# A fifth of two FFN weights placed on partitions 0 to 63 and loaded by eight of the sixteen DMA engines, in a decode kernel that is bound by its DMA engines

## The chip, the cores and the metric

The kernel runs on one core of a Trainium2 chip. The metric is the device time of one execution in microseconds (us). Where a ratio is given, it is the mean time of one kernel's fast runs over that of the other kernel's fast runs of the same rounds on the same chip, so it is not quite the ratio of the medians quoted beside it.

## The reference

One decode step of a parallel block: attention over the last 2,048 positions of a K and a V cache, plus a gated FFN, plus the residual. Everything is bf16.

```python
# x [4,1,640]; k_cache, v_cache [4,32,8192,192]; wq [640,6144]; wo [6144,640]
# w1, w3 [640,1536]; w2 [1536,640]; window W = 2048
xn = layernorm(x)
out = x + attention(xn @ wq, k_cache[:, :, -W:], v_cache[:, :, -W:]) @ wo \
        + (silu(xn @ w1) * (xn @ w3)) @ w2
```

The data is 223 MB, nearly all K and V, read once. There is little arithmetic per byte.

## The kernel before

All loads are issued from one queue (SP), in program order. K tiles have two buffers, V tiles three; wq borrows the V buffers at the start. VectorE (DVE) multiplies K by the broadcast query, TensorE (PE) adds up by matmul with the identity, and so on. The parts that matter here:

```python
def load_k(h):                      # 128 partitions x 24,576 bytes
    kt = kpool.tile([P, NJ, Dh], BF16, tag="kt")
    nc.sync.dma_start(out=kt[:].rearrange("q j d -> q (j d)"),
                      in_=k_win[:, h].rearrange("b (p j) d -> p b (j d)", p=PB))
# ... load_v alike
def x_load():                       # x a second time, for the residual
    xr["t"] = const.tile([B, D], BF16, name="x_res")
    nc.sync.dma_start(out=xr["t"][:], in_=A_x.rearrange("b s d -> (b s) d"))
# ...
def ffn_load(name, w):              # w1, w3: 128 partitions x 5 rows of 3,072 bytes
    wt = fpool.tile([P, KC, F], BF16, tag="w", name=name)
    nc.sync.dma_start(out=wt[:].rearrange("p k n -> p (k n)"),
                      in_=w.rearrange("(p kc) n -> p (kc n)", kc=KC))
def ffn_in(name):
    for kc in range(KC):
        for w in range(HG):         # 4 column groups of 32
            nc.tensor.matmul(ffn["ps"][w*CT:(w+1)*CT, :], lhsT=xnT[:, kc]...[:, 0:CT],
                             rhs=ffn[name][:, kc, w*FW:(w+1)*FW], ...)
# schedule: w1 loaded in head 6, w3 in head 8; a slot is a quarter of a head
add(f, 0, ffn_load, "w1", B_w1)     # f = 6 * 4
add(f + 8, 0, ffn_load, "w3", B_w3)
```

Of the kernel before, what the change touches and what calls it, by code (L numbers as in the profile page):

```python
# [11 lines left out]
BF16 = mybir.dt.bfloat16  # L12
# [6 lines left out]
def kernel(  # L19
# [20 lines left out]
    nc = tc.nc  # L40
    P = 128
    B, Sq, D = A_x.shape
    _, H, Sk, Dh = A_k_cache.shape
    W = min(4096, max(256, Sk // 4))
    F = B_w1.shape[1]
    KC = D // P
# [9 lines left out]
    CT = 32  # L56
# [3 lines left out]
    N0 = D // 2  # L60
    QC = 512
    NQ = H * Dh // QC
    assert D % P == 0 and F % QC == 0 and P % B == 0 and W % (PB * GQ) == 0
    assert JQ * DD == 512 and JQ % 2 == 0 and 2 * Dh <= 512 and 2 * N0 == D and N0 <= 512
    assert (H * Dh) % QC == 0 and NQ % 6 == 0 and QW % P == 0 and Dh == CT * RPP and P == HG * CT and F == HG * CT * FC
    assert 2 * H * Dh <= NJ * Dh and KBUFS == 2 and VBUFS == 3
# [3 lines left out]
    fpool = ctx.enter_context(tc.tile_pool(name="ffn", bufs=1))  # L70
# [3 lines left out]
    const = ctx.enter_context(tc.tile_pool(name="const", bufs=1))  # L74
# [5 lines left out]
    ps_t = ctx.enter_context(tc.tile_pool(name="ps_t", bufs=1, space=MemoryType.PSUM))  # L80
# [29 lines left out]
    x_sb = const.tile([B, D], BF16, name="x_sb")  # L110
# [3 lines left out]
    for k0 in range(0, KC, 2):  # L114
        n = min(2, KC - k0)
        wt = vpool.tile([P, 2, H * Dh], BF16, tag="vt")
        nc.sync.dma_start(out=wt[:, 0:n, :].rearrange("p k n -> p (k n)"),
                          in_=wq_v[:, k0:k0 + n, :].rearrange("p k n -> p (k n)"))
# [4 lines left out]
    idb = const.tile([P, P], BF16, name="idb")  # L123
# [38 lines left out]
    xn = const.tile([B, D], BF16, name="xn")  # L162
# [6 lines left out]
    xnT = const.tile([P, KC, PB, B], BF16, name="xnT")  # L169
    nc.vector.tensor_copy(out=xnT[:], in_=xnT_ps[:].unsqueeze(2).to_broadcast([P, KC, PB, B]))  # L170


    qbc = const.tile([P, H * Dh], BF16, name="qbc")
    for c0 in range(0, NQ, 6):
        qps = [pool.tile([P, QC], FP32, tag=tag, name="qps")
               for pool, tag in ((ps_add, "ps"), (ps_add, "ps"), (ps_o, "o_ps"), (ps_o, "o_ps"), (ps_m, "mt"), (ps_t, "t"))]
        for kc in range(KC):
            for i, qp in enumerate(qps):
                nc.tensor.matmul(qp[:], lhsT=xnT[:, kc].rearrange("p a b -> p (a b)"),  # L179
                                 rhs=wq_rows[kc][:, (c0 + i) * QC:(c0 + i + 1) * QC],  # L180
                                 start=(kc == 0), stop=(kc == KC - 1))
# [17 lines left out]
    def acc_half(i, lhsT, rhs, first=False, last=False):  # L199
        nc.tensor.matmul(acc[i * CT:i * CT + B, :], lhsT=lhsT, rhs=rhs[:, i * N0:(i + 1) * N0], start=first, stop=last)  # L200
# [3 lines left out]
            acc_half(i, lhsT, rhs, last=last)  # L204

    po = ps_po.tile([P, Dh + 1], FP32, name="po")
    xr = {}

    def x_load():
        xr["t"] = const.tile([B, D], BF16, name="x_res")  # L210
        nc.sync.dma_start(out=xr["t"][:], in_=A_x.rearrange("b s d -> (b s) d"))

    def x_add(i):
        acc_half(i, idb[0:B, 0:B], xr["t"], first=True)

    def mult(u):
        h, g = u // GQ, u % GQ
# [106 lines left out]
    FW = F // HG  # L324
# [3 lines left out]
    ffn = {}  # L328

    def ffn_load(name, w):  # L330
        wt = fpool.tile([P, KC, F], BF16, tag="w", name=name)
        nc.sync.dma_start(out=wt[:].rearrange("p k n -> p (k n)"), in_=w.rearrange("(p kc) n -> p (kc n)", kc=KC))
        ffn[name] = wt

    def ffn_in(name):
        ffn["ps"] = ps_t.tile([P, FW], FP32, tag="t", name="f_ps")
        for kc in range(KC):
            for w in range(HG):
                nc.tensor.matmul(ffn["ps"][w * CT:(w + 1) * CT, :], lhsT=xnT[:, kc].rearrange("p a b -> p (a b)")[:, 0:CT],
                                 rhs=ffn[name][:, kc, w * FW:(w + 1) * FW], start=(kc == 0), stop=(kc == KC - 1))  # L340

    def ffn_silu():
        nc.scalar.activation(out=sT[:], in_=ffn.pop("ps")[:], func=ACTF.Silu)
# [23 lines left out]
    def add(slot, phase, fn, *args):  # L367
        sched[slot].append((phase, len(sched[slot]), fn, args))
# [31 lines left out]
    e = ends[H - 1][1] + 1  # L400
    for hg in range(NG - 2):
        a = ((hg + 1) * HG - 1) * GQ + L + 3
        add(hg * HG * GQ + 8, 0, wo_load, hg)
        add(a, 6, ge_proj, hg, 0, RPP // 2)
        add(a + 1, 6, ge_proj, hg, RPP // 2, RPP)
    f = FFN_HEAD * GQ
    add(f, 0, ffn_load, "w1", B_w1)
    add(f + 7, 7, ffn_in, "w1")
    add(f + 7, 9, ffn_silu)
    add(f + 8, 0, ffn_load, "w3", B_w3)  # L410
    add(f + 15, 7, ffn_in, "w3")
    add(f + 15, 9, ffn_h)
    add(8, 0, x_load)
    add(16, 6, x_add, 0)
    add(17, 6, x_add, 1)


# [53 lines left out]
```

## Time and profile before

| | before |
|---|---|
| median of the first runs | 529.32 us |
| span of the profiled execution | 527.6 us |
| DMA | 423 GB/s mean, 9 tenths busy or more in all slices but two |
| PE, DVE busy | 67%, 65% |

First, lines of the profile page of the kernel before: the busy time of each engine (PEld is TensorE loading weights, ACT is ScalarE, POOL is GpSimd); the DMA share in tenths over 40 equal slices of the span and what the engines moved; the DMA queues (packets, MB, share of the time of 16 engines); and the chain of work that ended last, by line.

```profile
PE 353.5 (67%) x2306; PEld 142.6 (27%) x2307; DVE 345.6 (65%) x435; ACT 45.6 (9%) x143; POOL 1.1 (0%) x8
DMA  8999999999999999999999999999999999999994
GB/s 358 434 430 415 420 439 434 430 434 419 439 438 427 432 427 437 429 434 428 432 432 432 432 427 435 432 432 430 432 430 432 432 430 434 429 435 427 438 419 203
q1 hardware_dynamic: 11680, 222.97, 98.6%
q8 instruction: 18, 0.29, 0.2%
q14 instruction: 5, 0.04, 0.0%
DMA kt<-in_A_k_cache_dram 54%; DVE pr L219 15%; PE ps L230 9%; PE po L307 4%; DVE sc L238 3%; DMA wt<-in_A_wq_dram 3%; PE qps L179 2%; PE o_ps L282 2%; DVE z L274 1%; ACT ex L266 1%; PE mt L260 1%; DVE oT L315 1%; DVE og L312 0%; PE acc L200 0%; ACT L266 0%
```

The kernel's own queue q1 fills 98.6% of what sixteen engines have, and the chain is mostly waits for K tiles. So no engine of the core but the DMA engines limits it. The two "instruction" queues look negligible by bytes. They are not: they don't fall evenly on the sixteen engines.

Now the timeline of the kernel before at four places (start in us, length, engine, line, operation, and in brackets the idle time before it and what ended it): where PE starts on wq, where DVE starts on the last K tile, one matmul group of the tail, and the last matmuls and the last DVE instruction.

```profile
10.70 4.89 PE L179 MATMUL qps<-wt,xnT 128*128 128x512 bf16 x12 [2.35 <-DMA wt<-in_A_wq_dram]
498.64 1.76 DVE L219 TENSOR_TENSOR pr<-kt,qbc 128x3072 bf16<-128x3072 bf16 x1 [2.71 <-DMA kt<-in_A_k_cache_dram]
513.82 2.73 PE L282 MATMUL o_ps<-vt,z 128*8 128x384 bf16 x32
523.86 0.71 PE L200 MATMUL acc<-w,hT 128*4 128x320 bf16 x8
524.62 0.48 DVE L437 CAST res<-acc 36x320 bf16<-36x320 f32 x1 [1.62 <-PE acc L200]
```

After the last K tile there are still 25 us of DMA (V, wo, w2) and 26 us of compute, side by side.

**A view that the argument needs.** The trace also records every DMA packet and every increment of a DMA's semaphore (the counter by which an engine that waits learns that a load has landed). A K load has sixteen increments in the trace of before, the second load of x (four rows) has four. Each is taken here as one engine's share landing: three of the increments come 2.52, 2.67 to 2.69 and 2.80 to 2.82 us after the first in each of the loads that land from 481, 488 and 495 us on. A tile counts as landed at the last one (DVE starts on the last K tile at 498.64 us, 0.02 us after its last increment). For the last K tile of the kernel before, in us after the first engine:

```
first engine 495.43:  0  0.25 0.26 0.26 0.36 0.39 0.77 | 2.52 2.68 2.81 3.08 3.08 3.10 3.11 3.11 3.20   -> lands at 498.62
```

Seven engines are early, nine late. All sixteen had started level, within 0.5 us at 43 us. What holds nine back can be followed in the packets: when q8 brings one of its 18 packets of 16 KB (0.88 to 0.97 us each), one engine loses about 1.45 us (the packet itself, and 0.45 to 0.55 us by which the data packet beside it gets longer than its 912 ns). Eight engines take turns in this. A ninth gets three packets of 8 KB on q14 and loses about 0.8 us by each (0.31 us for the packet, 0.53 or 0.54 us by which a data packet gets longer). These packets keep step with the program: q8 brings 18 for 4,613 instructions of PE and PEld, one for about 256, and the three of q14 come when 50, 178 and 303 of DVE's recorded instructions have begun. This is why they are called "DVE fetches".

### The profile page before, as it was taken

The numbers are of one execution on the slowest core, as the hardware profiler recorded it, in microseconds if no ns is written. First come the engines' busy times: TensorE is split into PE (matmuls) and PEld (weight loads), VectorE is DVE, ScalarE is ACT, GpSimd is POOL, SyncE is SP. The second block draws the span as 40 slices with busy tenths as digits, with TensorE's granted clock in tenths as the row PEclk, the third lists the DMA queues.
The fourth block names the chain that finished last, engine by engine and source line by source line (L and its number), as shares of the span: only waits on it lengthen the run. The fifth ranks groups of instructions, "written<-read, shape, count | busy, mean of one in ns | idle before, by whom it ended". The sixth has DMA issues, their size and how long they took to land.

```text
span 527.6 us, 5428 instructions
## 1 busy us (share of the span) xinstructions
PE 353.5 (67%) x2306; PEld 142.6 (27%) x2307; DVE 345.6 (65%) x435; ACT 45.6 (9%) x143; POOL 1.1 (0%) x8
## 2 busy tenths in 40 slices
PE   2865886765657476577637866577566777675686
PEld 0322332322212232223212322223222332232233
DVE  3179775776458567686637876577657867677661
ACT  2111000100211000000000000000000000000010
POOL 0000000000000000000000000000000000000000
PEclk9889887899878989789997998789997988799788
DMA  8999999999999999999999999999999999999994
GB/s 358 434 430 415 420 439 434 430 434 419 439 438 427 432 427 437 429 434 428 432 432 432 432 427 435 432 432 430 432 430 432 432 430 434 429 435 427 438 419 203
DMA packets 11719, 223.31 MB, mean 423 GB/s; under 512 B 1312, under 2 KB 1328, under 8 KB 2608
## 3 DMA queue, kind: packets, MB, share of 16 engines
q1 hardware_dynamic: 11680, 222.97, 98.6%
q8 instruction: 18, 0.29, 0.2%
q14 instruction: 5, 0.04, 0.0%
q10 hardware_dynamic: 16, 0.01, 0.0%
HBM read 222.96 MB, written 0.01 MB: 423 GB/s over the span
## 4 chain that ended last, share of the span: by engine, by line
DMA 57%; DVE 22%; PE 18%; ACT 2%; issue 1%; SPq 0%
DMA kt<-in_A_k_cache_dram 54%; DVE pr L219 15%; PE ps L230 9%; PE po L307 4%; DVE sc L238 3%; DMA wt<-in_A_wq_dram 3%; PE qps L179 2%; PE o_ps L282 2%; DVE z L274 1%; ACT ex L266 1%; PE mt L260 1%; DVE oT L315 1%; DVE og L312 0%; PE acc L200 0%; ACT L266 0%
## 5 line engine op out<-in xcount | busy, mean ns | idle before, releaser
L230 PE MATMUL ps<-pr,idb 128*128 128x512 bf16 x768 | 208.5, 412 | 152.3 <-DVE pr L219 152.3
L219 DVE TENSOR_TENSOR pr<-kt,qbc 128x3072 bf16<-128x3072 bf16 x128 | 223.5, 1746 | 113.9 <-DMA kt<-in_A_k_cache_dram 113.9
L230 PEld LDWEIGHTS <-idb 128*128 128x128 bf16 x768 | 74.4, 102 | 258.7 <-issue 200.1
L238 DVE TENSOR_REDUCE sc<-ps 128x16 f32<-128x512 f32 x128 | 87.2, 681 | 2.0 <-PE ps L230 2.0
L282 PE MATMUL o_ps<-vt,z 128*8 128x384 bf16 x1024 | 60.6, 373 | 2.7 <-DMA vt<-in_A_v_cache_dram 2.7
L307 PE MATMUL po<-o_sb,sel_w 128*32 128x192 f32 x128 | 49.1, 517 | 1.1 <-ACT o_sb L289 1.1
L282 PEld LDWEIGHTS <-z 128*8 128x8 bf16 x1024 | 26.2, 94 | 32.8 <-issue 22.8
L289 ACT COPY o_sb<-o_ps 128x384 f32<-128x384 f32 x32 | 15.3, 479 | 189.7 <-PE o_ps L282 189.7
L274 DVE TENSOR_TENSOR z<-ex,mask_b 128x256 bf16<-128x256 bf16 x32 | 13.5, 422 | 22.0 <-ACT ex L266 22.0
L263 ACT COPY negm<-mt 128x1 f32<-128x1 f32 x32 | 5.1, 159 | 259.0 <-PE mt L260 259.0
L307 PEld LDWEIGHTS po<-o_sb,sel_w 128*32 128x32 f32 x128 | 13.6, 128 | 26.8 <-issue 25.0
L179 PE MATMUL qps<-wt,xnT 128*128 128x512 bf16 x59 | 17.2, 456 | 4.8 <-DMA wt<-in_A_wq_dram 4.7
L185 DVE CAST qbc<-qps 128x512 bf16<-128x512 f32 x6 | 3.8, 684 | 18.7 <-PE qps L179 18.7
L260 PEld LDWEIGHTS mt<-ones_ff,gneg 1*128 1x128 f32 x64 | 9.5, 186 | 13.8 <-issue 11.7
L252 DVE TENSOR_REDUCE gmax<-mt 1x4 f32<-1x128 f32 x32 | 8.8, 275 | 6.6 <-PE mt L247 6.6
L260 PE MATMUL mt<-ones_ff,gneg 1*128 1x1 f32 x64 | 12.2, 258 | 0.0
L247 PE MATMUL mt<-idf,lmax 128*1 128x128 f32 x32 | 10.6, 330 | 1.1 <-DVE lmax L242 1.1
L266 ACT ACTIVATE ex<-sc,negm 128x64 bf16<-128x64 f32 x32 | 11.1, 348 | 1.0
L179 PEld LDWEIGHTS <-xnT 128*128 128x128 bf16 x60 | 6.7, 112 | 14.8 <-issue 9.7
L200 PE MATMUL acc<-wo_t,oT 128*4 128x320 bf16 x96 | 9.2, 298 | 0.4 <-DVE oT L315 0.4
L294 PEld LDWEIGHTS po<-rsum,tot_w 128*32 128x32 f32 x64 | 4.6, 110 | 14.1 <-issue 12.5
L242 DVE TENSOR_REDUCE lmax<-sc 128x1 f32<-128x64 f32 x32 | 7.0, 220 | 1.1
(52 smaller groups left out, 64.2 us busy)
## 6 DMA issues: line engine op xcount, KB each, us to landing
kt<-in_A_k_cache_dram SPq DMA_DIRECT2D x32, 3072.0 KB, 19.0
vt<-in_A_v_cache_dram SPq DMA_DIRECT2D x31, 3072.0 KB, 26.1
wo_t<-in_A_wo_dram SPq DMA_DIRECT2D x8, 960.0 KB, 20.5
wt<-in_A_wq_dram SPq DMA_DIRECT2D x2, 3072.0 KB, 13.3
w<-in_B_w_dram SPq DMA_DIRECT2D x2, 1920.0 KB, 27.1
vt<-in_A_v_cache_dram SPq DMA_DIRECT2D x2, 1536.0 KB, 31.2
wt<-in_A_wq_dram SPq DMA_DIRECT2D x1, 1536.0 KB
w<-in_B_w_dram SPq DMA_DIRECT2D x1, 1280.0 KB, 33.6
```

The lines of the kernel that those rows point to most:

```text
L179: nc.tensor.matmul(qp[:], lhsT=xnT[:, kc].rearrange("p a b -> p (a b)"), rhs=wq_rows[kc][:, (c0 + i) * QC:(c0 + i + 1) * QC], start=(kc == ...
L200: nc.tensor.matmul(acc[i * CT:i * CT + B, :], lhsT=lhsT, rhs=rhs[:, i * N0:(i + 1) * N0], start=first, stop=last)
L219: nc.vector.tensor_tensor(out=pr[:], in0=kts[h][:, g * JQ:(g + 1) * JQ, :], in1=qbc[:, h * Dh:(h + 1) * Dh].unsqueeze(1).to_broadcast([P, ...
L230: nc.tensor.matmul(ps[:], lhsT=idb[:], rhs=pr[:, :, kk * DD:(kk + 1) * DD], start=(kk == 0), stop=(kk == NK - 1))
L238: nc.vector.tensor_reduce(out=scs[h][:, g * JQ:(g + 1) * JQ], in_=pss.pop(u)[:], axis=AX.X, op=ALU.add)
L247: nc.tensor.transpose(out=mt[0:1, 0:P], in_=chs[h][0][:], identity=idf[:])
L260: nc.tensor.matmul(mt[:, P:P + 1], lhsT=gneg[:].rearrange("o p b -> o (p b)"), rhs=ones_ff[0:1, 0:1], start=True, stop=True)
L266: nc.scalar.activation(out=ex[:], in_=scs.pop(h)[:], func=ACTF.Exp, bias=negm[:, 0:1], scale=SCALE, accum_out=rsum[:])
L274: nc.vector.tensor_tensor(out=z[:], in0=ex[:].unsqueeze(2).to_broadcast([P, NJ, B]), in1=mask_b[:].unsqueeze(1).to_broadcast([P, NJ, B]), ...
L282: nc.tensor.matmul(o_ps[c * CT:c * CT + 2 * B, :], lhsT=z[:, 2 * jj:2 * jj + 2, :], rhs=vt[:, 2 * jj:2 * jj + 2, :], start=(jj < 4), stop= ...
L289: nc.scalar.copy(out=o_sb[:], in_=o_ps[:])
L307: nc.tensor.matmul(po[sl, 0:Dh], lhsT=sel_w[:, par].rearrange("p a b -> p (a b)"), rhs=o_sb[:, par * Dh:(par + 1) * Dh].rearrange("p (r i) ...
```

## The change

The intent: put a fifth of w1 and w3 on eight DMA engines alone (called the low ones below), and so relieve the eight others (the high ones). The weights keep four rows on each of 128 partitions; the last 128 rows go two to a partition on partitions 0 to 63, in two loads of 32 partitions. The source of these is viewed as 8 x 4 rows, strided, so that the load is split into eight shares. The transposed x gets a copy in the matching row order. The second load of x goes. In the diff, cut to its core:

```diff
+    FA = KC - 1
+    FB = P // 2
...
+    xnF_ps = ps_t.tile([P, FA + 2, B], BF16, tag="t", name="xnF_ps")
+    for kc in range(FA):
+        nc.tensor.transpose(out=xnF_ps[:, kc, :], in_=xn[:, kc:FA * P:FA], identity=idb[0:B, 0:B])
+    xnB = const.tile([B, 2, FB], BF16, name="xnB")
+    for kc in range(2):
+        nc.vector.tensor_copy(out=xnB[:, kc, :].rearrange("b (w e a) -> b w e a", a=4, e=8),
+                              in_=xn[:, FA * P + kc:D:2].rearrange("b (w a e) -> b w e a", a=4, e=8))
+        nc.tensor.transpose(out=xnF_ps[0:FB, FA + kc, :], in_=xnB[:, kc, :], identity=idb[0:B, 0:B])
+    xnF = ...                        # two copies from PSUM
...
-        acc_half(i, idb[0:B, 0:B], xr["t"], first=True)
+        acc_half(i, idb[0:B, 0:B], x_sb, first=True)
...
-        wt = fpool.tile([P, KC, F], BF16, tag="w", name=name)
-        nc.sync.dma_start(out=wt[:].rearrange("p k n -> p (k n)"), in_=w.rearrange("(p kc) n -> p (kc n)", kc=KC))
+        wt = fpool.tile([P, FA + 2, F], BF16, tag="w", name=name)
+        nc.sync.dma_start(out=wt[:, 0:FA, :].rearrange("p k n -> p (k n)"),
+                          in_=w[0:FA * P, :].rearrange("(p kc) n -> p (kc n)", kc=FA))
+        w_b = w[FA * P:D, :].rearrange("(p kc) n -> p (kc n)", kc=2)
+        for r in range(0, FB, CT):
+            nc.sync.dma_start(out=wt[r:r + CT, FA:FA + 2, :].rearrange("p k n -> p (k n)"),
+                              in_=w_b[r:r + CT, :].rearrange("(a e) n -> e a n", e=8))
...
-        for kc in range(KC):
+        for kc in range(FA + 2):
+            n = P if kc < FA else FB   # matmuls on 128 or on 64 rows
...
-    add(8, 0, x_load)
```

More of the change, by code (lines that the diff above doesn't have):

```diff
@@ L170 @@
     nc.vector.tensor_copy(out=xnT[:], in_=xnT_ps[:].unsqueeze(2).to_broadcast([P, KC, PB, B]))
+    xnF_ps = ps_t.tile([P, FA + 2, B], BF16, tag="t", name="xnF_ps")
[6 more added lines that the diff above has]
+        nc.tensor.transpose(out=xnF_ps[0:FB, FA + kc, :], in_=xnB[:, kc, :], identity=idb[0:B, 0:B])
+    xnF = const.tile([P, FA + 2, CT // B, B], BF16, name="xnF")
+    nc.vector.tensor_copy(out=xnF[:, 0:FA], in_=xnF_ps[:, 0:FA].unsqueeze(2).to_broadcast([P, FA, CT // B, B]))
+    nc.vector.tensor_copy(out=xnF[0:FB, FA:FA + 2], in_=xnF_ps[0:FB, FA:FA + 2].unsqueeze(2).to_broadcast([FB, 2, CT // B, B]))
     qbc = const.tile([P, H * Dh], BF16, name="qbc")
@@ L206 @@
     po = ps_po.tile([P, Dh + 1], FP32, name="po")
-    xr = {}
-    def x_load():
-        xr["t"] = const.tile([B, D], BF16, name="x_res")
-        nc.sync.dma_start(out=xr["t"][:], in_=A_x.rearrange("b s d -> (b s) d"))
     def x_add(i):
-        acc_half(i, idb[0:B, 0:B], xr["t"], first=True)
+        acc_half(i, idb[0:B, 0:B], x_sb, first=True)
     def mult(u):
@@ L336, in ffn_in @@
         ffn["ps"] = ps_t.tile([P, FW], FP32, tag="t", name="f_ps")
-        for kc in range(KC):
+        for kc in range(FA + 2):
+            n = P if kc < FA else FB
             for w in range(HG):
-                nc.tensor.matmul(ffn["ps"][w * CT:(w + 1) * CT, :], lhsT=xnT[:, kc].rearrange("p a b -> p (a b)")[:, 0:CT],
-                                 rhs=ffn[name][:, kc, w * FW:(w + 1) * FW], start=(kc == 0), stop=(kc == KC - 1))
+                nc.tensor.matmul(ffn["ps"][w * CT:(w + 1) * CT, :], lhsT=xnF[0:n, kc].rearrange("p a b -> p (a b)"),
+                                 rhs=ffn[name][0:n, kc, w * FW:(w + 1) * FW], start=(kc == 0), stop=(kc == FA + 1))
     def ffn_silu():
```

## The prediction

> **What bounds the kernel now.** The DMA engines. The page's slices show them 9 tenths busy or more in every slice but the first and last, at 427 to 439 GB/s; queue q1 alone fills 98.6% of 16 engines' span, and the chain of waits is 54% K-cache loads. PE (67%) and DVE (65%) have slack. A 24,576-byte packet takes 912 ns, in nearly all of 8,320 cases, so an engine needs about 516 us for its 13.9 MB of a 527.6 us span. Bytes don't change, so only the balance between engines can pay.
>
> **How uneven the engines are.** I read this from the packets (chained into 16 sequences by size and time) and from each load's 16 landing times. The engines start level (0.5 us spread at 43 us). Instruction fetches then hold single engines back: queue q8 brings 16 KB about every 29 us, about 1.5 us each, in turn on eight engines; queue q14 brings 8 KB, about 0.8 us each time, three times (57, 218, 365 us) on one other engine. When the last K tile lands (first engine 495.43, last 498.62 us), seven engines stand at 0 to 0.77 us, the q14 engine at 2.54, the eight q8 engines at 2.7 to 3.2 us. DVE starts on that tile at once (498.64), and everything after it is a chain of compute; the last w2 part lands at 523.85, just inside that chain.
>
> The old reload of x (four partitions) used four engines[...]. Three are fast ones; the fourth is the q14 engine. So the low eight are, I take it, the seven fast ones plus the q14 engine, and the q8 engines are 8 to 15.
>
> **What the change does.** [...] Per weight a high engine now carries 8 packets of 12,288 bytes (460 ns, as the wq half load shows) instead of 8 of 15,360 (573 ns): -0.9 us. A low one has in addition 8 of 6,144 bytes, by interpolation (estimate) 234 ns, and two semaphore writes: +1.0 us. Both weights: high -1.8, low +2.0 us. [...]
>
> At the last K tile, on the old scale: high engines 0.9 to 1.4, seven low ones 1.9 to 2.7, the q14 engine 2.54 + 2.0 - 0.15 = about 4.4 us, against a latest of 3.2 before. The intent overshoots on one engine: the tile lands about 1.1 us later, and the compute tail moves with it.
>
> **Other costs.** Six transposes and four small copies at 9 to 10 us: PE then waits for wq until 10.70 us, so hidden. Eight more FFN matmuls of 384 columns[...]: PE slack. One DMA wait less on SP; four more issues, hidden, since loads wait 19 to 26 us in the queue.
>
> **Predicted: 530.3 us, range 528.4 to 531.3. Faster by over 2%: 0.01; within 2%: 0.98; slower by over 2%: 0.01.**
>
> **What would show it.** Landings of the last K tile: one straggler near 4.4 us behind the old first engine, eight others early; 6,144-byte packets on eight engines alone; DVE's first multiply of the last head about 1 us later; about the same q8 and q14 fetches.
>
> **What would make it wrong.** If the q14 engine weren't among the low eight, or its fetches moved, the latest engine would be at 2.7 us: about 0.6 us faster. If the K tile's landing had slack, no change. A startup stall at 10 us would add up to 1 us.

The four and the eight engines of two loads were taken to be the lowest ones. That these engines are the lowest was the assumption: the traces show four increments for the load of x (before) and eight for each small load (after), no numbers. The sum keeps the term of x as its - 0.15: it came to about 4.4 us for the latest landing, about 1.1 us later than before, and to 530.3 us in all. The traces show 55 ns for each of the four packets of x (before) and 326 ns in the median for an FFN matmul (after). The packets of 4 bytes, read here as semaphore writes, took 9 ns each: after has 28 more of them than before, as its four small loads add 32 increments and the load of x no longer makes four.

## The result and the profile after

| | before | after |
|---|---|---|
| first rounds, median (range) | 529.31 (529.07 to 529.55) | 529.93 (529.45 to 530.96), ratio 1.0014 [0.9997, 1.0032] |
| again, on another chip, 5 rounds | 529.29 (529.04 to 530.39) | 530.06 (529.26 to 531.86), ratio 1.0006 [0.9992, 1.0020] |
| profiled execution | 527.6 | 529.0 |

The medians are 0.6 and 0.8 us higher, 0.1 to 0.15%, but both intervals include no change, so the loss is not shown by these times alone. The traces below show what happens inside. The profiled execution of after was the slowest of its four (530.96 us; that of before took 529.69), so the difference at its end is larger than that of the medians. Lines of the page after, then the issues of the weight loads (count, KB each, median us from issue to landing where it could be told):

```profile
PE 353.4 (67%) x2321; PEld 142.6 (27%) x2321; DVE 346.1 (65%) x439; ACT 45.6 (9%) x143; POOL 1.1 (0%) x8
q1 hardware_dynamic: 11832, 222.96, 98.3%
w<-in_B_w_dram SPq DMA_DIRECT2D x2, 1536.0 KB, 29.1
w<-in_B_w_dram SPq DMA_DIRECT2D x4, 192.0 KB
```

The bytes are the same, and each weight has now three loads. The timeline after, at the start (what the change adds there) and at the places shown of before:

```profile
8.80 0.33 DVE L180 COPY xnB<-xn 4x64 bf16<-4x64 bf16 x2
8.94 0.26 PE L177 MATMUL xnF_ps<-idb,xn 4*128 4x4 bf16 x4 [0.58 <-DVE xnT L172]
9.13 0.26 PE L182 MATMUL xnF_ps<-idb,xnB 4*64 4x4 bf16 x2
10.71 4.35 PE L193 MATMUL qps<-wt,xnT 128*128 128x512 bf16 x12 [1.31 <-DMA wt<-in_A_wq_dram]
500.51 1.76 DVE L227 TENSOR_TENSOR pr<-kt,qbc 128x3072 bf16<-128x3072 bf16 x1 [3.07 <-DMA kt<-in_A_k_cache_dram]
515.56 2.60 PE L290 MATMUL o_ps<-vt,z 128*8 128x384 bf16 x32
525.48 0.71 PE L214 MATMUL acc<-w,hT 128*4 128x320 bf16 x8
526.23 0.48 DVE L450 CAST res<-acc 36x320 bf16<-36x320 f32 x1 [1.62 <-PE acc L214]
```

The added transposes and copies are over by 9.7 us, and PE still waits for wq until 10.71, as before (10.70). The last K tile is used at 500.51 instead of 498.64, 1.87 us later, and the end follows: `res` comes 1.61 us later. The landings of the last K tile:

```
before  495.43: 0 0.25 0.26 0.26 0.36 0.39 0.77 2.52 2.68 2.81 3.08 3.08 3.10 3.11 3.11 3.20                -> 498.62
after   493.66: 0 0.49 | 2.32 2.80 2.81 2.91 2.94 2.95 | 3.64 4.01 4.11 4.13 4.30 | 6.20 6.59 6.83          -> 500.49
```

The third K load was issued at 41.10 us before and at 41.08 after, so the shift does not come from the start. The first engine is 1.77 us earlier, as meant. But three engines, not one, are left far behind. Two of them can't be the q14 engine.

### The profile page after: what moved, and what is told of

Its sections match the earlier page's. It is cut to its first block, busy times and chain, and to the rows that moved or that the text cites. A ratio compares the mean times of both kernels' runs of the same rounds, so it can differ in the third digit from the quotient of the medians.

```text
span 529.0 us, 5465 instructions
## 1 busy us (share of the span) xinstructions
PE 353.4 (67%) x2321; PEld 142.6 (27%) x2321; DVE 346.1 (65%) x439; ACT 45.6 (9%) x143; POOL 1.1 (0%) x8
## 2 busy tenths in 40 slices
DMA packets 11871, 223.30 MB, mean 422 GB/s; under 512 B 1340, under 2 KB 1352, under 8 KB 2760
## 4 chain that ended last, share of the span: by engine, by line
DMA 57%; DVE 22%; PE 18%; ACT 2%; issue 1%; SPq 0%
DMA kt<-in_A_k_cache_dram 54%; DVE pr L227 15%; PE ps L238 9%; PE po L315 4%; DVE sc L246 3%; DMA wt<-in_A_wq_dram 3%; PE qps L193 2%; PE o_ps L290 2%; DVE z L282 1%; ACT ex L274 1%; PE mt L268 1%; DVE oT L323 1%; DVE og L320 0%; PE acc L214 0%; ACT L274 0%
## 5 line engine op out<-in xcount | busy, mean ns | idle before, releaser
L238 PE MATMUL ps<-pr,idb 128*128 128x512 bf16 x768 | 211.6, 417 | 153.8 <-DVE pr L227 153.7
L290 PE MATMUL o_ps<-vt,z 128*8 128x384 bf16 x1024 | 57.1, 357 | 3.0 <-DMA vt<-in_A_v_cache_dram 3.0
L290 PEld LDWEIGHTS <-z 128*8 128x8 bf16 x1024 | 25.5, 91 | 31.0 <-issue 20.1
L315 PEld LDWEIGHTS po<-o_sb,sel_w 128*32 128x32 f32 x128 | 13.7, 129 | 27.4 <-issue 25.6
```

The source lines that it names most:

```text
L238: nc.tensor.matmul(ps[:], lhsT=idb[:], rhs=pr[:, :, kk * DD:(kk + 1) * DD], start=(kk == 0), stop=(kk == NK - 1))
L290: nc.tensor.matmul(o_ps[c * CT:c * CT + 2 * B, :], lhsT=z[:, 2 * jj:2 * jj + 2, :], rhs=vt[:, 2 * jj:2 * jj + 2, :], start=(jj < 4), stop= ...
L315: nc.tensor.matmul(po[sl, 0:Dh], lhsT=sel_w[:, par].rearrange("p a b -> p (a b)"), rhs=o_sb[:, par * Dh:(par + 1) * Dh].rearrange("p (r i) ...
```

## The experiments

Two theories were on the table. **A** (the prediction's): the eight engines with the q8 packets are 8 to 15, the low eight hold only the q14 engine as a slow one. **B**: the q8 engines straddle the line, two of them are among the low eight, and the change loads what was already the latest. A third, **C**: the engines of these packets change each time the program is loaded.

### Which engine is which: tiny loads as markers

```diff
+    def marker(k):
+        mk = small.tile([16, 128], BF16, tag="mk", bufs=2, name="mk")
+        nc.sync.dma_start(out=mk[0:k, :], in_=A_wq[0:k, 0:128])
...
+    for k in range(1, 16):
+        add((15 + k) * GQ + 2, 0, marker, k)
```

> The kernel before with fifteen tiny loads (k rows of 256 bytes, k = 1 to 15, one for each of the heads 16 to 30)[...], to tell which engine stands where. Theory A (as predicted): engines 0 to 7 hold the seven fast ones and the engine with the DVE fetches (about 2.5 us behind at the end), engines 8 to 15 are all the ones slowed by the q8 fetches. Theory B (from the profile after, where two of the eight engines with 6,144-byte packets had 1.6 and 1.9 us at 132 us already): the q8 fetches fall on a set of eight engines that straddles the line, two of them in 0 to 7, in the kernel before too. Theory C: the set changes from load to load of the program. Time within 0.5 us of before.

> The changed kernel with the same fifteen tiny loads. Theory B: the same engines as in the run with markers on the kernel before, two low ones 6 to 7 us behind the first engine at the last K tile, and about 1.3 us slower than before in the profiled run. Theory C: another set, and the delay of the last K tile goes with how many q8 engines lie among the low eight: about 1.1 us later than before with none, about 1.9 us with one or more.

Each marker of k rows lands with exactly k increments. The list for k and that for k - 1 differ by one engine, which is called number k - 1 here. Some of the lists of the kernel before with markers, in us after the first increment of the list:

```
k = 4   0 0.09 0.76 1.46                                          (342 us)
k = 6   0 0.08 0.33 0.77 2.42 2.64                                (371 us; a q14 packet came at 365)
k = 8   0 0.07 0.09 0.34 0.79 2.31 2.63 2.89                      (402 us)
k = 9   0 0.33 0.38 0.42 0.67 1.11 2.61 2.94 3.21                 (417 us)  a new first one: engine 8 is early
k = 10  0 0.32 0.38 0.42 0.67 1.11 2.61 2.94 2.95 3.20            engine 9 late; the same for 10 to 14
k = 15  0 0.32 0.36 0.40 0.64 1.10 2.60 2.80 2.81 2.83 2.89 2.93 2.94 2.96 3.17
all 16  0 0.07 0.31 0.32 0.39 0.62 1.09 2.59 2.80 2.81 2.84 2.90 2.90 2.94 2.95 3.14    engine 15 is the 0.07
```

So among engines 0 to 7 five are early and three late: 3 (the one with the q14 packets: it is new at k = 4 and moves with the q14 packet at 365 us), 5 and 6. Late above are 9 to 14; engines 8 and 15 are early. The changed kernel gave the same set: its list for k = 8 is 0, 0.28, 0.33, 0.81, 0.86, 2.76, 2.81, 3.09, its new one at k = 9 is earliest by 3.7 us, and the one that is missing at k = 15 is the second earliest. **Theory A falls, B holds, and C finds no support**: two kernels on one chip here, and on two other chips the changed kernel again had three stragglers. In the changed kernel with markers three engines end 6.38, 6.41 and 6.70 us behind the first at the last K tile (two had been expected, at 6 to 7). The expected times were no use: 530.56 and 530.63 us, and the first one is over 0.5 us above the median of before (the stall at 43 us, which comes below: its third K load was issued 1.05 us later than before's).

So the numbers are names, given in the order in which the markers add engines. That they are the chip's own numbers is not shown by a run here, and the argument does not need it: that the sets are nested and that the change loads three late engines is seen in the lists alone (in the trace of after, the first small load of w3 lands from 167.17 us on with 0, 0.10, 0.42, 0.51, 0.65, 0.91, 1.57 and 1.82 us, and in the loads that land from 210 to 317 us on three of the sixteen are 5.2 to 5.5 us behind).

### Dropping the second load of x alone

```diff
-        acc_half(i, idb[0:B, 0:B], xr["t"], first=True)
+        acc_half(i, idb[0:B, 0:B], x_sb, first=True)
-    add(8, 0, x_load)
```

> The kernel before with only the second load of x dropped. Both theories: within 0.3 us of before[...].

529.50 us against 529.76, ratio 1.0001 [0.9982, 1.0020]. As expected, nothing that can be told apart.

### The same rows, spread over all sixteen engines

```diff
-        for r in range(0, FB, CT):
-            nc.sync.dma_start(out=wt[r:r + CT, FA:FA + 2, :].rearrange("p k n -> p (k n)"),
-                              in_=w_b[r:r + CT, :].rearrange("(a e) n -> e a n", e=8))
+        nc.sync.dma_start(out=wt[0:FB, FA:FA + 2, :].rearrange("p k n -> p (k n)"), in_=w_b[:, :])
```

(with the copy of x in plain order)

> The changed kernel with the fifth of w1 and w3 still on partitions 0 to 63 but in one load of 64 rows each, so that all 16 engines carry it; everything else of the change kept. If the loss is the uneven share of the engines: as before, within 0.3 us, and the last K tile lands about 3.2 us after the first engine, as before. If it is the added transposes, copies, matmuls or issues: as slow as the change, 0.6 us over before.

Both expectations missed, so this run can't separate the uneven share from the other parts of the change (the useless loads below do): 535.37 us against 529.76, ratio 1.0100 [1.0080, 1.0119], 5.6 us slower. Its two loads have sixteen increments each by the count of packets under 512 bytes: 1,340, as in the trace of after with four loads of eight. The last K tile lands at 505.44. The loss comes in the two stretches in which these rows are loaded. The table by stretches, columns: stretch, length, busy time of PE, PEld, DVE, ACT, POOL (with counts), granted clock, DMA share, GB/s. First the changed kernel, then this one:

```profile
128.00:142.00 14.00, 9.77 (x57) 3.79 (x57) 9.58 (x12) 2.37 (x5) 0.00 (x0) 0.88 1.02 437
164.00:178.00 14.00, 13.15 (x110) 5.24 (x110) 12.63 (x15) 1.08 (x4) 0.00 (x0) 0.88 1.03 444
```

```profile
128.00:142.00 14.00, 9.08 (x57) 3.62 (x57) 9.68 (x12) 2.37 (x5) 0.00 (x0) 1.00 1.02 352
164.00:178.00 14.00, 11.72 (x95) 4.77 (x94) 12.63 (x17) 1.08 (x4) 0.00 (x0) 0.88 1.02 348
```

The engines are just as busy and move a fifth less. In the packet records a 6,144-byte packet takes 412 ns in the median here and 234 ns in the changed kernel, and 24,576-byte packets of the neighbouring loads take up to 2.05 us instead of 0.91. So with twice as many engines into the same 64 partitions a packet takes almost twice the time (1.76 times). Why is not shown by a run here. But the odd form of the change, two loads of 32 partitions with eight shares each, is not decoration: in it these packets take 234 ns, what an estimate gives for 6,144 bytes from the 102 ns of 2,560 and the 291 ns of 7,680 in the trace of before.

### The stall at 43 us, and an early w1

The runs of one kernel differ by up to 2.9 us (x_only), too much for what is sought. The traces show one place where they differ: at about 43 us the DMA queue runs dry, since the third K load waits for DVE's first tile (in the trace of before DVE's last multiply of it ends at 41.08 us and the load is issued at 41.10), and how late that is goes roughly with the granted clock (the share of TensorE's full clock that the profile shows as granted). In the seven traces with this order of loads the issue was at 40.33 and 41.09 us at a granted clock from 10 to 42 us of 0.95, at 41.08, 41.10 and 41.14 at 0.89, at 42.15 at 0.84 and at 43.21 at 0.79. To bridge it, w1 was issued right behind the first two K loads:

```diff
-    add(f, 0, ffn_load, "w1", B_w1)
+    add(0, 0, ffn_load, "w1", B_w1)
```

> The kernel before with the load of w1 issued first in the loop, right after the first two K loads, instead of at head 6. The DMA queue ran dry at about 43 us in every run so far, for about 0.5 to 2 us, by an amount that varies from run to run; w1's 4.6 us of transfer should bridge it. If this stall is where the spread of the runs comes from: 0.5 to 1.5 us faster than before, and a spread of the runs below 0.5 us. If not: as before, spread as before.

> The changed kernel with the same early w1. Theory B (engines 5 and 6, slowed by q8 fetches, get 1.9 us more, and the last K tile waits for them): 1.6 to 2.0 us slower than early. If the change costs only the 0.6 us that the medians showed: 0.6 us slower. If the compute tail has slack: equal.

The stretch 42 to 45 us (columns as above) in the kernel before, in the slow one of these traces (the changed kernel, second time), and with the early w1:

```profile
42.00:45.00 3.00, 2.15 (x10) 0.85 (x9) 2.97 (x4) 0.00 (x0) 0.00 (x0) 1.00 0.80 311
```

```profile
42.00:45.00 3.00, 1.68 (x8) 0.58 (x6) 3.00 (x3) 0.00 (x0) 0.00 (x0) 1.00 0.23 79
```

```profile
42.00:45.00 3.00, 2.15 (x10) 0.85 (x9) 2.96 (x4) 0.00 (x0) 0.00 (x0) 1.00 0.95 410
```

The stall is gone, and in its trace the last K tile lands at 498.17, 0.45 us earlier than in the trace of before. The five runs agree within 0.66 us (528.75 to 529.41, median 529.08; below 0.5 had been expected), against 1.55 us for nine of before (528.58 to 530.13, median 529.37). But the changed kernel with the early w1 still spreads over 1.38 us (528.96 to 530.34), so the stall is not the only source. The expected gain of 0.5 to 1.5 us was not there: 0.3 us in the medians, ratio 0.9995 [0.9983, 1.0008]. Why so little shows in its tail, where PE waits for the last part of w2:

```profile
513.29 1.47 PE L282 MATMUL o_ps<-vt,z 128*8 128x384 bf16 x32
523.28 0.44 PE L200 MATMUL acc<-w,hT 128*4 128x320 bf16 x4 [0.51 <-DMA w<-in_B_w_dram]
523.76 0.48 DVE L437 CAST res<-acc 36x320 bf16<-36x320 f32 x1 [2.54 <-PE acc L200]
```

The same 32 matmuls take 1.47 us here and 2.73 us in the trace of before: the granted clock from 514 to 516 us was 1.00 here and 0.50 there. What makes the granted clock fall is not shown here. In this trace, with these matmuls at full clock, the compute is done earlier and the end is the last DMA landing (523.24), not the last K tile.

The change on this base costs 0.85 us in the medians (529.93 against 529.08, with ranges that overlap; against before the ratio is 1.0009 [0.9996, 1.0022]). Theory B's 1.6 to 2.0 us were missed: in the traces the last K tile comes 1.54 us later (499.71), but only a part of that reaches the medians.

### Useless loads: which engines have room

On the early base, one load that no result uses, at head 16. The first two versions took the rows in plain order:

```diff
+    def extra():
+        dm = fpool.tile([P, KC * F], BF16, tag="w", name="dm")
+        nc.sync.dma_start(out=dm[0:4 * 3, 0:H * Dh], in_=A_wq[0:4 * 3, :].rearrange("(e a) n -> e a n", e=3))
```

> early with a useless load of 12 rows of 12,288 bytes at head 16, on engines 0, 1 and 2 alone (four packets, 1.84 us each; no result uses it). Theory B has these three among the engines that are only 0 to 1 us behind the first at the last K tile, against 3.2 for the latest: within 0.3 us of early. If any load added to an engine delays the end: 1.8 us slower.

> The same with 32 rows on engines 0 to 7, again four packets and 1.84 us on each. Theory B: engines 5 and 6 are in it and are the latest already, so 1.6 to 1.9 us slower than early. Theory A (engines 8 to 15 are the latest, only the one with the DVE fetches low): about 1.1 us slower.

These failed as experiments, and the landings say why: the first load has twelve increments and the second sixteen. So they ran on 12 and 16 engines, into 12 and 32 partitions; it looks as if the dims "(e a)" in plain order, which are contiguous, counted as one of 12 or 32 rows. And as with sixteen engines before, packets were slow: those beside these loads took up to 1.95 us. They cost 1.1 and 3.5 us against early (530.22 and 532.63; against before the ratios are 1.0016 [1.0004, 1.0029] and 1.0064 [1.0050, 1.0078]). They say nothing about A and B, but they are a second and a third case of what the sixteen-engine version showed. With the rows strided, as the change does it:

```diff
-        ...A_wq[0:4 * 8, :].rearrange("(e a) n -> e a n", e=8))
+        ...A_wq[0:4 * 8, :].rearrange("(a e) n -> e a n", e=8))
```

> The useless load again, now with its rows taken in a strided order, as the change does (rows a*3+e for engine e), so that it can't be merged and does run on engines 0, 1 and 2 alone[...]: four packets of 12,288 bytes, 1.84 us each. Theory B: these engines stand 0 to 1.1 us behind the first at the last K tile, the latest 3.0 to 3.3, so within 0.4 us of early (529.1). If any added load delays the end: 1.8 us slower.

> The same on engines 0 to 4. Theory B has the DVE fetches on engine 3 (2.5 to 2.8 us behind): the last K tile lands at about 2.7 + 1.8 = 4.5 instead of 3.3 us, so 1.0 to 1.4 us slower than early, between the run with three and the run with eight engines.

> The same on engines 0 to 7. Theory B: engines 5 and 6 are among the latest already (about 3.0), so the last K tile lands at 4.8 to 5.0 instead of 3.3 us, 1.5 to 1.8 us slower than early. Theory A (no q8 engine among the low eight): as with five engines.

Now the loads have 3, 5 and 8 increments, all 460 ns a packet, and no packet beside them is slow. (That these are the engines 0 to 2, 0 to 4 and 0 to 7 of the markers is inferred; the landings below fit it.) The two runs with eight (early_x8 and early_k8) also make a clean comparison for what the sixteen-engine version showed: the same 32 rows go into the same 32 partitions, on sixteen engines with packets of up to 0.98 us, on eight with 0.46 us. DVE's start on the last K tile with early, and with the loads on 0 to 2, 0 to 4 and 0 to 7:

```profile
498.19 1.76 DVE L219 TENSOR_TENSOR pr<-kt,qbc 128x3072 bf16<-128x3072 bf16 x1 [3.97 <-DMA kt<-in_A_k_cache_dram]
498.09 1.76 DVE L219 TENSOR_TENSOR pr<-kt,qbc 128x3072 bf16<-128x3072 bf16 x1 [2.61 <-DMA kt<-in_A_k_cache_dram]
499.34 1.76 DVE L219 TENSOR_TENSOR pr<-kt,qbc 128x3072 bf16<-128x3072 bf16 x1 [2.89 <-DMA kt<-in_A_k_cache_dram]
499.57 1.76 DVE L219 TENSOR_TENSOR pr<-kt,qbc 128x3072 bf16<-128x3072 bf16 x1 [4.01 <-DMA kt<-in_A_k_cache_dram]
```

The landings of that tile, against the 498.17 of early (first engine 494.86, latest 3.30):

| load on | landings, latest ones | last K tile | against early | median (early: 529.08) |
|---|---|---|---|---|
| 0 to 2 | 3.06, 3.15, 3.19 | 498.07 | -0.10 | 528.69 |
| 0 to 4 | 2.88, 2.93, then one at 4.33 | 499.32 | +1.15 | 529.51 |
| 0 to 7 | 3.40, then three at 4.71, 4.77, 4.79 | 499.55 | +1.38 | 529.66 |

For the landings this is theory B within 0.2 us: three engines carry 1.84 us more (four packets of 460 ns) at no cost (a step of 0.1 us down is noise), five bring up one straggler (predicted 4.5), eight bring up three (predicted 4.8 to 5.0). By theory A the eight would have had one straggler, as the five. The medians follow only in part: +0.4 and +0.6 us for 1.15 and 1.38 us at the tile, short of the 1.0 to 1.8 us that had been expected. The medians of early and of these three come from different chips, so the better comparison is among the three: the loads on 0 to 4 and on 0 to 7 cost 0.82 and 0.97 us in the medians against the load on 0 to 2 (tile: 1.25 and 1.48 us later), and every run of theirs (529.35 to 530.23, 529.10 to 530.61) is slower than every run of it (528.56 to 528.94). So in the time too a load costs more when late engines carry a share of it; with the three early ones alone no cost shows. Five against eight can't be told apart by time; there only the landings decide between A and B. Against before the ratios are 0.9985 [0.9973, 0.9998], 1.0003 [0.9990, 1.0015] and 1.0004 [0.9991, 1.0018].

Here are the tails of the profiled executions, from DVE's start on the last K tile to the last DVE instruction:

| trace | start to `res`, us | 32 matmuls of the tail | held by |
|---|---|---|---|
| before | 25.98 | 2.73 us (half clock) | compute |
| after | 25.72 | 2.60 | compute |
| early with the change | 25.86 | 2.73 | compute |
| load on 0 to 4 | 25.99 | 2.73 | compute |
| load on 0 to 7 | 24.63 | 1.47 | compute |
| after, second time | 24.60 | 1.47 | compute |
| early | 25.57 | 1.47 | wait of 0.51 for w2 |
| load on 0 to 2 | 25.77 | 1.47 | wait of 0.29 for w2 |

So the compute after the last K tile takes 24.6 us or 25.5 to 26.0 us (25.5 is the load on 0 to 2 without its wait; its half-clock stretch lies before the 32 matmuls, from 495 to 506 us), as the clock happens to be granted (a mean of 0.88 over the two tails of 24.6 us, of 0.85 to 0.87 over the four of 25.7 to 26.0 us that compute holds), and the end is the later of that and of the last w2 landing. A K tile that is on time has about 1 us to spare when the tail takes 24.6 us (instead of 25.6); a late one has none. This fits the medians' losing only a part of the delay. It is shown for these eight traces; that the executions without a trace mix the two cases is inferred.

### The changed kernel again

> The changed kernel once more, on this chip and beside the others. Theory B: the last K tile's landings again have three engines of the low eight at 6.2 to 6.9 us behind the first, and the tile lands 1.5 to 1.9 us later than it does before; 0.6 to 1.5 us slower in the median, since the tail and the stall at 43 us vary by about 0.5 us each. Theory C (the engines of the fetches change from load to load): another pattern.

530.06 us against 529.29, ratio 1.0006. In its trace the stall was the longest seen, so the whole is late (last K tile at 502.54), but the pattern is the same: after the first engine 0.13, 1.56, then eight engines at 2.76 to 3.23, then 3.68 and 3.73, and three at 5.64, 5.80 and 5.86 (6.2 to 6.9 had been expected). That the tile would be 1.5 to 1.9 us later than before can't be read from it, since its stall is 2 us longer than in the trace of before.

## Why the prediction was right, and where it was not

It gave 530.3 us (528.4 to 531.3) and "within 2%"; measured were 529.93 and 530.06. The direction, a small loss, was right in the medians, though their intervals include no change. The size was less than predicted: 0.6 to 0.8 us in place of 1.0. Step by step:

- **What bounds the kernel**: right. The K tiles' landings set the pace to 500 us (in the trace of before DVE waits 113.9 us for them in 29 waits).
- **How uneven the engines are**: right in the numbers (nine late engines, the q8 packets 1.45 us each, the q14 engine at 2.5 us).
- **"So the low eight are, I take it, the seven fast ones plus the q14 engine, and the q8 engines are 8 to 15"**: this step failed. It was an inference from four engines to eight, on the assumption that the lowest are used. The markers show five early ones, the q14 engine and two q8 engines (5 and 6) among the low eight, and two early ones (8 and 15) above.
- **What is moved**: right. High engines predicted 1.8 us earlier, the first one was 1.77. On the old scale the q14 engine was predicted at about 4.4; if it is the first of the three late ones, it stands at 493.66 + 6.20 - 495.43 = 4.43. The latest landing moved by 1.87 us (predicted for low engines: 2.0).
- **"the tile lands about 1.1 us later"**: it landed 1.87 us later, because of the two engines not reckoned with.
- **"and the compute tail moves with it"**: true in the trace, from the slowest of four runs (1.61 us at the end), only in part in the medians. In the tails of early and of the load on 0 to 2 PE waited 0.51 and 0.29 us for the last part of w2, so there a part of a delay is absorbed. The prediction had seen that w2 lands "just inside that chain", and had not asked what happens when the chain gets shorter.
- So two errors, one up and one down, partly cancelled. That the size came out nearly right was luck: the reason was not quite the stated one.
- **Other costs**: right. PE's start on wq did not move (10.70 and 10.71 us), and the load of x was worth nothing that could be measured.

If the q8 engines had been 8 to 15 as believed, the change should still have lost through engine 3, as the load on 0 to 4 did. Its idea is sound in so far as engines 0, 1 and 2 do have 1.8 us of room for free. What a load on these three could win is small: R us taken from each of the other thirteen are 13R/3 more for each of the three, and by the marker lists one of the three is the early engine at 0.77; 3.2 - R = 0.77 + 13R/3 gives R = 0.46 us (an estimate from the landings of before). It was not tried. The early w1 alone is 0.3 us below before in the medians and not told apart from it. With the useless load on 0 to 2 added it is 0.6 us below, with an interval that just excludes no change (0.9985 [0.9973, 0.9998]). The load itself is hardly the reason; whether the early w1 gains something stays open.

## What to carry to other kernels

Here, with all DMA engines full, a tile landed with its slowest engine: DVE started on the last K tile 0.02 us after the last of its sixteen increments. So look at the sixteen landings of the loads that are waited for, not at the mean share: an engine lost 3 us in 500 to packets that take 0.2% of the engines' time. Before moving load between engines, find out which of them a load will use and which are slow, with tiny marker loads of k rows (each landed with k increments here); it took one run. And the same rows into the same few partitions cost 0.6 us (eight shares) or 5.6 us (sixteen) here, so check how a load into few partitions is split.
